# Transposing the softmax of two recurrent layers with 80 columns into two PSUM banks, and a new order of TensorE's work

## The chip, the cores and the metric

The kernel runs on one core of a Trainium2 chip. The metric is the device time of one execution in microseconds; a comparison is a median of several runs. Before the change it is 2704.88 us, the median of three runs (2704.35 to 2705.86).

A core has five engines that matter here. PE (TensorE) multiplies matrices: it holds a stationary matrix, streams the moving one through it column by column, and writes to PSUM. PSUM has eight banks of 512 fp32 columns and 128 partitions. ACT (ScalarE) and DVE (VectorE) read PSUM and write SBUF, the working memory. POOL (GpSimd) clears buffers here. SP issues most of the DMAs. Every engine works through its own queue in order and waits on semaphores for the others.

## What is computed

Two transformer layers on a sequence of 2048 rows of 576 values. Each has a recurrent attention and a gated feed-forward part. The attention goes through the sequence in 64 segments of 32 rows; each segment sees its own rows and 8 memory rows, which are the first 8 rows of the attention's output on the segment before.

```python
for s in range(n_seg):
    h = concat([mem, x[s*32:(s+1)*32]])            # 40 rows
    q, k, v = h @ Wq, h @ Wk, h @ Wv               # 32 heads of 128
    p = softmax(where(mask, q @ k.T * scale, -1e9))
    o = (p @ v) @ Wo
    mem = o[:8]
    outs.append(o[8:])
x = x + A(layernorm(x)); x = x + B(layernorm(x))   # twice, with the same weights
```

B is `(silu(x @ w1) * (x @ w3)) @ w2` with 4608 inner columns.

## The kernel before

**Steps.** The second layer follows the first by 8 segments (`LAG`). Step t works on segment t of layer 1 and segment t - 8 of layer 2, so there are 72 steps: 56 with both layers (`both(t)`), 16 with one. Where both run, the 40 + 40 columns of the two segments lie beside each other, and most products have 80 moving columns. `role(t)` alternates between 0 and 1 from step to step; with it alternates the order in which memory and rows of the two layers stand in the buffers.

**One step.** It is worked in four groups of eight heads (`GH`). For each group PE makes Q and K (letters Q and q: the 512 rows of the contraction, and the last 64), the scores (S), a transpose of the softmax's result (T), P times V (P), and the product with Wo (O and o). Between S and T, DVE and ACT make the softmax: mask added, maximum subtracted, exponential, sum, and P itself, which DVE writes to `PB` in bf16 (`sm_pb`). Keys of the two layers go to different columns of `PB`, its 128 columns being the 128 rows of the tile V; the queries of layer kind 0 are in partitions 0 to 39, those of kind 1 in 64 to 103. What `sm_pb` doesn't write is zero, since POOL clears a buffer of `PB` after its use (`pb_zero`).

**The transpose** (`ptr`) is a matmul: the stationary side is one head's `PB` (104 rows, 128 columns), the moving side is `fold`, a matrix of 104 x 40 with ones that send row r and row 64 + r to the same column. The eight heads' results, 128 keys x 40 queries, fill 320 columns of one bank. Each key row belongs to one of the layers, so nothing is added twice.

**The two copies** (`pt_ev`) bring it to SBUF, to `PTS`. Where both layers run, each copy reads all 320 columns and multiplies each partition by 0 or 1 (`slots`, four masks of 128 x 1): one copy keeps the key rows of one layer, the other those of the other. P times V (`pv`) then takes both halves as its 80 moving columns, `PTS[:, i, 0:2, 40 columns]`. Where one layer runs there is no mask, and the two copies take 160 columns each. There is one buffer of `PTS`, so a transpose comes after the P times V before it.

**V, feed-forward.** V of a step, or of two steps at once, is made between (letters X, x, V, v, G, g) and evicted in strips of 32 or 64 rows. The feed-forward part (F, f, W, w) of a block of 128 rows, for one or two layers, is spread over the four steps after the block, and fills PE where attention waits.

**The order** of PE is written out by hand in `ORDER`, one letter for each piece of work (`KINDS`): `FIRST` (16 steps), `FOUR` (4 steps, eleven times) and `LAST` (12 steps and the end). The function `plan` follows this order for PE. For the other engines it takes, at each point, the ready piece with the lowest priority number, by durations that stand in `make_nodes`; pieces marked "AD" go to ACT or to DVE, whichever it finds free first. It also gives out the buffers: a piece takes (`acq`) banks and SBUF buffers when it starts, and gives them back (`rel`) when their last reader has ended. Waits on the chip follow from the data and the buffers so chosen; the planner's times only choose.

**Tiling modes.** PE works either at full width, in two halves of 64 columns ("col"), in rows of 64 ("row") or in smaller tiles. Each letter has one or two modes that it can use; one that can use the mode of the letter before it keeps it. The transpose and P times V can be "full" or "col"; in "col" each matmul is issued as two of 64 stationary columns.

**The recurrence.** After the last o of a step ACT and DVE add the two halves of the last 64 output columns (`y_odd` writes one half to `YO` in fp32), write the next memory to `HT` (`y_mem`) and the outputs to `YTS` (`yts`). Four segments later POST transposes `YTS` for the residual addition.

A matmul of any letter is issued by `mm`, an ACT operation by `act`, a DVE operation by `v`: so the profile shows the helpers' lines, L591 for PE, L594 for ACT, L597 for DVE, and L1010 for POOL's clearing.

Of the kernel before, what the change touches and what calls it, by code (L numbers as in the profile page):

```python
# [38 lines left out]
def role(t):  # L39

    return (t - LAG) % 2
# [152 lines left out]
def ewh(*ns):  # L194
# [5 lines left out]
    "maQQQqqQqqSQqTqSqQQQqSSvVXxPTPTOPOTOoPooOoQqqqqQQSQqqvSVQQTQSqqPQOTSPoXTOPToxPOOooQqqqqQQSQQSvqVQTqqQSQqPSaOTPTO"  # L200
    "PTooPOOooQQqqqqQSQVvSqqQQQqqQTSSPXTOPTOPoToxPOOooQQpQqqVvqqSnQQSfFFqqfQQqSTQqfPFTWPSFTOOooPFTffPOOooWQqqqqQQFSQF"
    "SQffqVvqqQWTQSFxfqfQFSPXTWPFTfOPOTFPOOooooWQqfqQQSFQfqqVvSQqqfFWTQqfQSFPQqfTOSPFOTWPFTOPfoooOoFfqqQQQSWQqqvVSFfq"
    "qQQTWqqSQQPTSOoPbaOTXPxTOPooxOoXqqpQQQSVqqnQvfFSTQqqQQPSFfqqfQTFOPSWTFfPOOTFPWOooooffFQQQqqqWSGFfgqQQqfFSTQPQQqq"
    "qfFSWGTSfgGPFggTGOPOTFPOOooooWVvfqqQQQSFqqffFQQWTSFfqqQPQfqqSFQWTOfPSTaFoOPWOTFPffFOoooWQQqqqqQSbQgqqGSQQTQPQTgq"
    "qSGSOPGggTGPOTOPoooOoQqqppQQQSvqqVnnQQqqSFSffqTFQPQqWTFSPffOwTFPOTFPOWOwooooFffqqQQQSWwQFfgqqGSFqqfQQTWQPQSFffqq"
    "FGTgSwPGfggTGPFTOPOWOOowoooFqqfQQwWQaQfqqSFSvVfqqQFQTFqqfPQTQwSWFSfPOOTFPwTWffFPOOooooWwqqqQQQbSQqqgqGSQTQPQQqgq"
    "TSGSGPggGTOPOTOPoooOo"
)
FOUR = (
    "QqqpQQpQqqVvnSSnQFfqfqFQQQTfqqSFPWTFPSwTfFOOPWTwPOOooooFqqffQQQQfqqSFGSgqfFTQQPwQTQqqqgGSWPFGSfggfFOTGPOwTOPWOoo"  # L210
    "ooFqfqqQQwWQQVqvSaSFFffqqQQwQQqqSTWSFPffTFOPWwTOFPffTOFPwWOooooFfqqqQQWQQSqqqQSQQbQqgqSTGGPSgTGPOTggGPOTwPOOoooo"
)
LAST = (
    "QQpQqqqQSqQpnQqqVvTSSnQFffqqFPQTOwPoSWTffFPFTOPOOoooFqqqfQQwWQQfqfSFSFqGQQqqgTQQPWwFqgfTSSGGPFfggfFTGOPOTWPOOwoF"
    "oooFfqqfQQQwvSqqVQQWQqqSFTSqfqQPQWTOPSwFTFPffOTOwPWOooooFFqqffQQwQQqqvSWVSFqqfQQTWPQTqqSVQvPOSTbOPxwOoTooPOoXqQp"
    "QpqqvVQSQqqnQnSQQqqFTSfqfPQTOPSFTFPOWTOPwOooooFqffqQQQSQQqqqvVSTQQqqFSffqFPQWSwTFPffTOPFOTwPOOoWoooFqfqqQQQFSQfq"
    "xvXVwWSTFPQffqqQWQTSwFFPfqqQOSwWTFOPffTFPOWOwooooFQQvfqqVqqQSQWFSwFffqqQQQSTWQqPqTPSOTOPowOToboPxOoXqqqQQQpSvVqq"
    "qQQSnQTFfqQFSPfqQOSTFfPowTFPfOTOPFOfooowQQqqqfQQSqFSVvqqQwQFTSQffqqQPFTSXPwTOPOTFPOOooooFfxfVvqqQQQSQqqqfQSFQqqq"
    "QSTQwSPFTOffPFTOPwTOPfooOooFQqqqQQSqqqQQSQvVQTSfFQqqPwTFSPfTOFPOTOPoofOoopwFnfffFFwFwfffFFFwffFFwffFFwffFFwfFffF"
    "wFwfffFFFfww"  # L220
# [11 lines left out]
def make_nodes(em, nseg, pools, o=Opt, dma_bw=230e3, load_bw=400e3):  # L232
# [26 lines left out]
    ld_m0 = node("ACT", 0.1, em.load_m0(), prio=-90, name="m0", lat=2.5)  # L259
    ld_t = [load("ldt", kb(3 * R64, 4096), -10.0, em.load_tails(0)), node("ACT", 0.1, em.load_tails(1), prio=-120, name="ldt", lat=6.0)]  # L260
    node("ACT", 0.1, em.load_tails(2), prio=-80, name="ldt", lat=6.0)
# [48 lines left out]
    def v_nodes(name, t, k, prio, tail_at, emit, strips, deps, tail_deps, free):  # L310

        modes = ("col", "quad") if strips[0][3] == R64 else ("c32", "oct")
        b = banks()
        m_ = node("PE", 8 * 0.2158, emit(b, False), deps=deps, prio=prio, mode=modes[0], acq=b, name=name)
        n = node("PE", 0.2158, emit(b, True), deps=deps + tail_deps, prio=prio + tail_at, mode=modes[1], acq=b, name=name + "t")
        reads_ht.setdefault(t, []).extend([m_, n])
        for r in (0, 1):
            outs = em.v_parts(strips, r)
            b[r].users = len(outs)
            for p0, width, row, blk in outs:  # L320
                e = node("AD", (0.49, 0.6), em.v_ev(b[r], p0, width, row, blk), deps=[m_, n] + free.get(blk // 2, []), prio=prio + 0.01 * (blk // 2),
                         rel=[b[r]], name=name + "e")
                vx_ev.setdefault((name, t, blk // 2), []).append(e)
        return [m_, n]
# [16 lines left out]
    def vg_out(t, g, b, deps, row):  # L341

        return [node("AD", (0.49, 0.6), em.v_ev(b[r], row, R64, row, 2 * g + r), deps=deps, prio=t + o.vm + 0.01 * g + (0.05 if row == 0 else 0.0), rel=[b[r]],
                     name="VGe") for r in (0, 1)]

    def vx_pair(t, prio):

        if t and paired(t - 1):
            return
        deps = [ht_ready[li, s] for s in (t, t + 1) if 0 <= s < nst for li in layers_of(s) if s == t or li or not both(t)] + (ld_v if t <= 0 else [])  # L350
        free = {g: [pvs[t - 1, g]] for g in range(NG) if (t - 1, g) in pvs}
        for k in ((0, 1) if both(t) else (0,)):
            v_nodes("VX", t, k, prio + 0.01 * k, o.vxt, (lambda k: lambda b, tail: em.vx(t, k, b, tail))(k), em.vx_strips(t, k), deps, [], free)

    def step(t):
# [17 lines left out]
        for g in range(NG):  # L373
# [52 lines left out]
            me[f"SC{g}"], me[f"TR{g}"], me[f"PV{g}"], me[f"WO{g}"] = sc, tr, pv, wo  # L426
# [100 lines left out]
    def x_in(g):  # L527
        xn = Slot("xn")
        ld = node("DMA" if g else "ACT", 0.8 if g else 0.1, em.load_xn(g, xn), deps=reads_ht.get(4 * g - 3, [])[:1], prio=4 * g - 3.0 if g else -100, acq=[xn],
                  name="ldxn", lat=2.5)  # L530
# [37 lines left out]
class Emitter:  # L568
# [431 lines left out]
    def sm_pb(self, t, g, sme, pb):  # L1000
        def f(n):
            for kd, key, c0, w in self.p_at(t):
                rs = slice(64 * kd, 64 * kd + QW)
                X, rec = self.T.SME[rs, sme.i], self.T.STAT[rs, sme.i]
                self.v("tensor_tensor", self.T.PB[rs, pb.i, :, c0:c0 + w], X[:, :, key:key + w],
                       rec.unsqueeze(2).to_broadcast([QW, GH, w]), op=ALU.mult)
        return f

    def pb_zero(self, pb):
        return lambda n: self.ch("POOL", self.nc.gpsimd.memset(self.T.PB[:, pb.i], 0.0))  # L1010
# [101 lines left out]
    def yts(self, t, ls, tail):  # L1112
        def f(n):
            yT, _ = self.yT(t)
            for li in ls:
                j = (t - LAG * li) % 4
                c0 = self.ycol(t, self.kind(t, li), False)
                if not tail:
                    self.cp(n, self.T.YTS[:, li, 0:4, j * SEG:(j + 1) * SEG], yT[:, 0:4, c0:c0 + SEG])
                else:  # L1120
                    self.v("tensor_tensor", self.T.YTS[R64:P, li, 4, j * SEG:(j + 1) * SEG], yT[0:R64, 4, c0:c0 + SEG],
# [3 lines left out]
    def post_tr(self, li, g, b):  # L1125
        def f(n):

            for db in (4, 3, 2, 1, 0):
                d0 = min(db * P, D - P)
                self.mm(self.bk_bf(b, D)[:, d0:d0 + P], self.T.YTS[:, li, db, :], self.T.ident[:, 0:P], True, True, is_transpose=True)  # L1130
# [79 lines left out]
def kernel(  # L1210
# [41 lines left out]
    T.fold = sp.tile([P, QW], BF, name="fold")  # L1252

    T.slots = sp.tile([P, 2, 2], F32, name="slots")

# [29 lines left out]
    nc.gpsimd.memset(T.fold[:], 0.0)  # L1285
    for r in (0, R64):
        nc.gpsimd.affine_select(out=T.fold[:], in_=T.fold[:], compare_op=ALU.not_equal, fill=1.0, base=-r,
                                pattern=[[-1, QW]], channel_multiplier=1)

    nc.gpsimd.memset(T.slots[:], 0.0)  # L1290
    for e, kd, lo, hi in ((0, 1, 24, 80), (1, 0, 72, 112)):
        inside, outside = T.slots[:, e, kd:kd + 1], T.slots[:, e, 1 - kd:2 - kd]
        nc.gpsimd.memset(inside, 1.0)
        nc.gpsimd.affine_select(out=inside, in_=inside, compare_op=ALU.is_ge, fill=0.0, base=-lo, pattern=[[0, 1]], channel_multiplier=1)
        nc.gpsimd.affine_select(out=inside, in_=inside, compare_op=ALU.is_ge, fill=0.0, base=hi - 1, pattern=[[0, 1]], channel_multiplier=-1)
        nc.gpsimd.tensor_scalar(outside, inside, -1.0, 1.0, op0=ALU.mult, op1=ALU.add)

# [54 lines left out]
```

## Time and profile before

| | |
|---|---|
| median of three runs | 2704.88 us |
| the profiled execution | 2708.0 us |
| its span | 2705.0 us |
| granted TensorE clock, mean | 0.997 |
| PE busy | 2618.6 us |
| DVE busy | 2097.7 us |
| ACT busy | 1401.6 us |
| DMA, mean | 119 GB/s |

The span goes from the first to the last instruction of one profiled execution. A group of instructions is given as engine, operation, what it writes and reads, shape and count; behind the bar stand its busy time, the mean duration in ns, and the idle time of its engine just before, with what ended it. "PE bank L591 <- ACT PTS L594" in a list of waits means that PE stood until ACT had written `PTS`; behind it stand the sum, the number of times and the longest. A matmul's duration holds its way through the array (about 0.18 us even for 40 columns), and the next one starts long before its end: what PE needs for a piece is read from start to next start.

### The profile page before, as it was taken

What the parts mean: (1) busy time and instruction counts of PE and PEld (TensorE: products, weight loads), DVE (VectorE), ACT (ScalarE), POOL (GpSimd) and SP (SyncE); (2) the same over time, 40 slices, a digit from 0 to 9 for tenths busy, and PEclk for the clock granted to TensorE, in tenths of its full rate; (3) what the DMA queues carried; (4) which work ended last, traced back from release to release, by engine and by line L of the source; (5) the groups of instructions that cost most, each with busy time, mean ns of one, the idle gap of its engine ahead of it and who ended that gap; (6) DMA issues with size and microseconds to landing.
All of it is one profiled execution on the core that took longest, in us unless ns stands there. A gap on an engine that the chain in (4) does not pass through costs nothing.

```text
span 2705.0 us, 135792 instructions
## 1 busy us (share of the span) xinstructions
PE 2618.6 (97%) x60482; PEld 2272.3 (84%) x60523; DVE 2097.7 (78%) x5423; ACT 1401.6 (52%) x3978; POOL 334.1 (12%) x411
## 2 busy tenths in 40 slices
PE   5999999999999999999999999999999999999998
PEld 4788888888888888888888888888888888888886
DVE  5777887787788778777877877787777777777876
ACT  2655554554555555554555555455545546554452
POOL 1111110110111011011101101010111101011110
PEclk9999999999999999999999999999999999999999
DMA  9064524244342434434243433423343342334457
GB/s 316 7 182 118 158 82 128 80 119 116 104 124 85 116 90 119 117 108 128 76 119 88 127 108 108 134 80 110 94 124 106 108 139 70 112 93 130 129 166 245
DMA packets 478171, 321.99 MB, mean 119 GB/s; under 512 B 26024, under 2 KB 467760, under 8 KB 476944
## 3 DMA queue, kind: packets, MB, share of 16 engines
q1 hardware_dynamic: 474048, 305.43, 38.5%
q8 instruction: 473, 7.75, 1.2%
q0 software_dynamic: 3024, 6.93, 0.9%
q10 hardware_dynamic: 512, 0.94, 0.2%
q14 instruction: 114, 0.93, 0.1%
HBM read 308.49 MB, written 2.36 MB: 115 GB/s over the span
## 4 chain that ended last, share of the span: by engine, by line
PE 80%; DVE 9%; ACT 6%; issue 2%; DMA 2%; SPq 1%; POOL 0%; ACTq 0%; DVEq 0%; POOLq 0%
PE bank L591 80%; ACT V L594 3%; DVE STAT L597 2%; DVE PTS L597 2%; ACT PTS L594 1%; DVE V L597 1%; DVE SME L597 1%; DVE PB L597 1%; DMA W<-in_A_Wk_dram 1%; DVE HTT L597 1%; SPq L600 1%; DMA W<-in_B_w_dram 1%; ACT HT L594 0%; ACT QKT L594 0%; DMA WV<-in_A_Wv_dram 0%
## 5 line engine op out<-in xcount | busy, mean ns | idle before, releaser
L591 PEld LDWEIGHTS <-W 128*128 128x128 bf16 (+2 forms) x31904 | 1258.2, 100 | 128.8 <-issue 68.7
L591 PE MATMUL bank<-HT,W 128*128 128x80 bf16 (+3 forms) x23040 | 799.9, 196 | 16.8 <-issue 7.3
L591 PE MATMUL bank<-XTB,W 128*64 128x256 bf16 (+5 forms) x8864 | 662.6, 263 | 5.9 <-DMA W<-in_B_w_dram 3.0
L594 ACT ACTIVATE QKT<-bank 128x256 bf16<-128x256 f32 (+2 forms) x1524 | 349.5, 311 | 363.5 <-PE bank L591 320.7
L1010 POOL MEMSET PB<- 128x1024 bf16 x288 | 273.9, 951 | 1944.5 <-PE bank L591 1242.7
L591 PE MATMUL bank<-OT,WO 128*128 128x80 bf16 (+2 forms) x11520 | 401.6, 198 | 2.2 <-issue 1.8
L594 ACT ACTIVATE V<-bank 32x512 bf16<-32x512 f32 (+1 forms) x609 | 347.8, 586 | 90.4 <-PE bank L591 81.6
L591 PEld LDWEIGHTS <-WO 128*128 128x128 bf16 (+1 forms) x11520 | 376.8, 102 | 13.7 <-issue 4.4
L591 PE MATMUL bank<-WV,HT 128*32 128x512 bf16 (+5 forms) x3728 | 362.3, 381 | 3.8 <-issue 2.2
L591 PE MATMUL bank<-W2C,HTT 128*128 128x288 bf16 (+1 forms) x2776 | 318.4, 286 | 2.9 <-issue 1.8
L597 DVE TENSOR_REDUCE STAT<-SME 104x8 f32<-104x320 f32 (+1 forms) x576 | 274.0, 476 | 25.2 <-ACT SME L594 18.9
L597 DVE TENSOR_TENSOR PB<-SME,STAT 40x128 bf16<-40x128 f32 (+4 forms) x912 | 275.5, 336 | 9.7
L594 ACT ACTIVATE HTT<-bank 128x512 bf16<-128x512 f32 (+1 forms) x324 | 175.3, 550 | 185.9 <-PE bank L591 183.9
L591 PEld LDWEIGHTS <-HT 128*32 128x32 bf16 (+4 forms) x3768 | 164.1, 99 | 119.5 <-issue 20.3
L597 DVE SCALAR_TENSOR_TENSOR XR<-bank,XR 128x288 f32<-128x288 f32 x576 | 243.7, 448 | 23.3 <-PE bank L591 17.4
L591 PEld LDWEIGHTS <-HTT 128*128 128x128 bf16 (+1 forms) x2840 | 222.4, 103 | 42.2 <-issue 4.5
L597 DVE SCALAR_TENSOR_TENSOR HTT<-HTT,bank 128x512 bf16<-128x512 bf16 (+1 forms) x324 | 201.0, 620 | 59.0 <-ACT HTT L594 56.2
L594 ACT ACTIVATE OT<-bank 128x320 bf16<-128x320 f32 (+1 forms) x392 | 147.0, 403 | 173.0 <-PE bank L591 146.3
L597 DVE CAST QKT<-bank 128x192 bf16<-128x192 f32 (+4 forms) x524 | 140.5, 315 | 117.7 <-PE bank L591 117.3
L597 DVE TENSOR_TENSOR HTT<-HTT,bank 128x512 bf16<-128x512 bf16 (+1 forms) x324 | 203.6, 628 | 28.5 <-PE bank L591 0.9
L594 ACT ACTIVATE PTS<-bank,slots 128x320 bf16<-128x320 f32 x315 | 157.0, 531 | 128.8 <-PE bank L591 95.0
L594 ACT ACTIVATE SME<-SME 104x320 f32<-104x320 f32 (+1 forms) x288 | 135.5, 470 | 100.2 <-DVE SME L597 95.5
(69 smaller groups left out, 1856.8 us busy)
## 6 DMA issues: line engine op xcount, KB each, us to landing
W<-in_B_w_dram SPq DMA_DIRECT2D x612, 256.0 KB, 3.6
W2C<-in_B_w_dram SPq DMA_DIRECT2D x306, 288.0 KB, 3.3
W<-in_B_w_dram SPq DMA_DIRECT2D x612, 32.0 KB, 3.5
W<-in_B_w_dram SPq DMA_DIRECT2D x8, 1024.0 KB, 12.2
W<-in_A_Wq_dram SPq DMA_DIRECT2D x9, 512.0 KB, 9.5
WO<-in_A_Wo_dram SPq DMA_DIRECT2D x4, 1152.0 KB, 16.7
XR<-in_A_x_dram POOLq DMA_DIRECT2D x16, 288.0 KB, 2.8
WV<-in_B_w_dram SPq DMA_DIRECT2D x4, 1152.0 KB, 10.9
```

The lines of the kernel that those rows point to most:

```text
L591: self.ch("PE", self.nc.tensor.matmul(out, lhsT=lhsT, rhs=rhs, start=start, stop=stop, skip_group_check=True, **k))
L594: self.ch("ACT", self.nc.scalar.activation(*a, **k))
L597: self.ch("DVE", getattr(self.nc.vector, fn_)(*a, **k))
L600: self.ch("SP", self.nc.sync.dma_start(out=out, in_=in_))
L1010: return lambda n: self.ch("POOL", self.nc.gpsimd.memset(self.T.PB[:, pb.i], 0.0))
```

## The change

- `ptr`: where both layers run, the moving side is now a part of the identity, 80 columns in two runs of 40 (columns 0 to 39 and 64 to 103 of `ident`, in the order that the step's role asks for). Each head gives 128 x 80, four heads fill 320 columns of a bank, eight heads take two banks. Key rows of one layer have zeros for the other layer's queries, from the zeros of `PB`. Where one layer runs, it is 40 columns and one bank, as before.
- `pt_ev`: plain copies of 320 columns, one for each bank: two where both layers run, one where one does. `PTS` has the eight heads in a row, 80 columns each, so P times V reads one run of 80.
- `fold` and `slots` go, with their building on POOL. `YO` has no memory of its own any more: it lies in partitions 0 to 63 of two blocks of `YTS`, whose other half holds the last 64 output columns. `YTS` is indexed anew for it.
- The planner's numbers: the transpose of 80 columns 0.0358 us a head, the copies by the formula `ew(320)`, the copies of V on ACT 0.56 for 0.49, and for the loads at the start larger costs, longer delays and a "boot" piece ahead of them on the DMA queue.
- `ORDER` has the same letters, as many of each, in another sequence.

```diff
 FOUR = (
-    "QqqpQQpQqqVvnSSnQFfqfqFQQQTfqqSFPWTFPSwTfFOOPWTwPOOooooFqqffQQQQfqqSFGSgqfFTQQPwQTQqqqgGSWPFGSfggfFOTGPOwTOPWOoo"
-    "ooFqfqqQQwWQQVqvSaSFFffqqQQwQQqqqSTWSFPffTFOPWwTOFPffTOFPwWOooooFfqqqQQWQQSqqqQSQQbQqqgqSTGGPSgTGPOTggGPOTwPOOoooo"
+    "QpQqqqqQpQvVnSSQnQFqffqFTQQfqqSFPWTFPSwffTFOPOOTWPwOooooFqfqqQQQQqgfSWFSFGqfqQQTQPQqqgTSGwPGSFTgffgFGOPOTwPOWOoo"
+    "ooFqqffQQQFQWqqVvwSSFqqfQQQQqqTSWPwSTFffPFOTwOPWFffTFPOOwoWaoooFqfqQQWSqqqQQQQSbQQqqgqGSSTGPgTGPOTggOPGTOPwOoooo"
 )
...
-            bt = Slot("bank", users=2)
-            tr = node("PE", 8 * 0.0258, em.ptr(t, g, pb, bt), deps=[pbs], prio=pf + o.tr, mode="full/col", acq=[pts, bt], name="TR")
+            bt = banks(nl)
+            tr = node("PE", 8 * (0.0258 if nl == 1 else 0.0358), em.ptr(t, g, pb, bt), deps=[pbs], prio=pf + o.tr, mode="full/col", acq=[pts] + bt, name="TR")
...
-            pe_ = [node("AD", (0.425, 0.46) if nl == 2 else ew(160), em.pt_ev(t, g, m, bt, pts), deps=[tr], prio=pf, rel=[bt], name="PTe") for m in (0, 1)]
+            pe_ = [node("AD", ew(320), em.pt_ev(t, g, i, b, pts), deps=[tr], prio=pf, rel=[b], name="PTe") for i, b in enumerate(bt)]
...
     def ptr(self, t, g, pb, b):
 
         def f(n):
+            nq, v, e = self.nq(t), self.T.ident[0:104, 0:1], role(t)
+            I = bass.AP(v.tensor, v.offset + R64 * e, [list(x) for x in v.ap][:-1] + [[R64 - P * e, 2], [1, QW]]) if nq == SW else self.T.ident[0:104, 0:QW]
             for j in range(GH):
-                self.mm(self.bk(b)[:, j * QW:(j + 1) * QW], self.T.PB[0:104, pb.i, j, :], self.T.fold[0:104, :], True, True)
-        return f
-
-    def pt_ev(self, t, g, m, b, pts):
-
-        def f(n):
-            src = self.bk(b)[:, 0:GH * QW]
-            if not self.both(t):
-                w = 4 * QW
-                self.cp(n, self.T.PTS[:, pts.i, 0, m * w:(m + 1) * w], src[:, m * w:(m + 1) * w])
-                return
-            dst = self.T.PTS[:, pts.i, m, :]
-            keep = self.T.slots[:, role(t), m ^ role(t):(m ^ role(t)) + 1]
-            if n.by == "ACT":
-                self.act(dst, src, ACT.Copy, scale=keep)
-            else:
-                self.v("tensor_scalar", dst, src, keep, None, op0=ALU.mult)
-        return f
+                k = j * nq % (4 * SW)
+                self.mm(self.bk(b[j * nq // (4 * SW)])[:, k:k + nq], self.pbt(pb)[0:104, j, :], I, True, True)
+        return f
+
+    def pt_ev(self, t, g, i, b, pts):
+        return lambda n: self.cp(n, self.T.PTS[:, pts.i, 4 * SW * i:4 * SW * (i + 1)], self.bk(b)[:, 0:4 * SW])
...
-                        self.T.PTS[:, pts.i, 0:nq // QW, j * QW:(j + 1) * QW], True, True)
+                        self.T.PTS[:, pts.i, j * nq:(j + 1) * nq], True, True)
...
-    T.PTS = sp.tile([P, pools["pts"], 2, GH * QW], BF, name="PTS")
+    T.PTS = sp.tile([P, pools["pts"], GH * SW], BF, name="PTS")
...
-    T.YO = sp.tile([R64, 2 * QW], F32, name="YO")
-    T.YTS = sp.tile([P, 2, 5, P], BF, name="YTS")
+    T.YTS = sp.tile([P, 10, P], BF, name="YTS")
+
+    T.YO = T.YTS[0:R64, 8:10, :].rearrange("p a b -> p (a b)").bitcast(F32)[:, 0:2 * QW]
```

More of the change, by code (lines that the diff above doesn't have):

```diff
@@ L257, in load @@
         return node("DMA", nbytes / load_bw, fn, deps=deps, prio=prio, name=name, lat=2.0)
-    ld_m0 = node("ACT", 0.1, em.load_m0(), prio=-90, name="m0", lat=2.5)
-    ld_t = [load("ldt", kb(3 * R64, 4096), -10.0, em.load_tails(0)), node("ACT", 0.1, em.load_tails(1), prio=-120, name="ldt", lat=6.0)]
-    node("ACT", 0.1, em.load_tails(2), prio=-80, name="ldt", lat=6.0)
+    node("DMA", 4.0, lambda n: None, prio=-999.0, name="boot")
+    ld_m0 = node("ACT", 0.6, em.load_m0(), prio=-90, name="m0", lat=8.0)
+    ld_t = [load("ldt", 1.7 * kb(3 * R64, 4096), -10.0, em.load_tails(0)), node("ACT", 0.6, em.load_tails(1), prio=-120, name="ldt", lat=8.0)]
+    node("ACT", 0.6, em.load_tails(2), prio=-80, name="ldt", lat=10.0)
     ld_h = [load("ldqk", kb(512, 4096), half - 9.0, em.load_qk(half)) for half in (0, 1)]
@@ L320, in v_nodes @@
             for p0, width, row, blk in outs:
-                e = node("AD", (0.49, 0.6), em.v_ev(b[r], p0, width, row, blk), deps=[m_, n] + free.get(blk // 2, []), prio=prio + 0.01 * (blk // 2),
+                e = node("AD", (0.56, 0.6), em.v_ev(b[r], p0, width, row, blk), deps=[m_, n] + free.get(blk // 2, []), prio=prio + 0.01 * (blk // 2),
                          rel=[b[r]], name=name + "e")
@@ L353, in vx_pair @@
             v_nodes("VX", t, k, prio + 0.01 * k, o.vxt, (lambda k: lambda b, tail: em.vx(t, k, b, tail))(k), em.vx_strips(t, k), deps, [], free)
+    last_pt = []
     def step(t):
@@ L528, in x_in @@
         xn = Slot("xn")
-        ld = node("DMA" if g else "ACT", 0.8 if g else 0.1, em.load_xn(g, xn), deps=reads_ht.get(4 * g - 3, [])[:1], prio=4 * g - 3.0 if g else -100, acq=[xn],
-                  name="ldxn", lat=2.5)
+        ld = node("DMA" if g else "ACT", 0.8 if g else 0.6, em.load_xn(g, xn), deps=reads_ht.get(4 * g - 3, [])[:1], prio=4 * g - 3.0 if g else -100, acq=[xn],
+                  name="ldxn", lat=2.5 if g else 9.0)
         ht_set(0, g, ln_nodes("L0", xn, xn, [ld], 4 * g - 2.0 if g else -8, ht_writes(0, g)))
@@ L1004, in f, with pbt @@
                 X, rec = self.T.SME[rs, sme.i], self.T.STAT[rs, sme.i]
-                self.v("tensor_tensor", self.T.PB[rs, pb.i, :, c0:c0 + w], X[:, :, key:key + w],
+                self.v("tensor_tensor", self.pbt(pb)[rs, :, c0:c0 + w], X[:, :, key:key + w],
                        rec.unsqueeze(2).to_broadcast([QW, GH, w]), op=ALU.mult)
         return f
+    def pbt(self, pb):
+        return self.T.PB[:, pb.i]
     def pb_zero(self, pb):
-        return lambda n: self.ch("POOL", self.nc.gpsimd.memset(self.T.PB[:, pb.i], 0.0))
+        return lambda n: self.ch("POOL", self.nc.gpsimd.memset(self.pbt(pb), 0.0))
     def nq(self, t):
@@ L1129, in f @@
                 d0 = min(db * P, D - P)
-                self.mm(self.bk_bf(b, D)[:, d0:d0 + P], self.T.YTS[:, li, db, :], self.T.ident[:, 0:P], True, True, is_transpose=True)
+                self.mm(self.bk_bf(b, D)[:, d0:d0 + P], self.T.YTS[:, 4 * li + db if db < 4 else 8 + li, :], self.T.ident[:, 0:P], True, True, is_transpose=True)
         return f
@@ L1250 @@
     T.ident = sp.tile([P, P], BF, name="ident")
-    T.fold = sp.tile([P, QW], BF, name="fold")
-    T.slots = sp.tile([P, 2, 2], F32, name="slots")
     T.maskb = sp.tile([P, 2, QW], BF, name="maskb")
@@ L1284 @@
                             pattern=[[-1, P]], channel_multiplier=1)
[L1285 to L1296, printed above, removed]
     nc.gpsimd.memset(T.maskb[:], 0.0)
```

39 lines of the change are left out of this document (19 added, 20 removed).

## The prediction

> **What bounds the kernel now.** I read the page first, for the engine shares and the chain.
>
> ```profile
> span 2705.0 us, 135792 instructions
> PE 2618.6 (97%) x60482; PEld 2272.3 (84%) x60523; DVE 2097.7 (78%) x5423; ACT 1401.6 (52%) x3978; POOL 334.1 (12%) x411
> PE 80%; DVE 9%; ACT 6%; issue 2%; DMA 2%; SPq 1%; POOL 0%; ACTq 0%; DVEq 0%; POOLq 0%
> ```
>
> PE is busy 97% of the span and holds 80% of the chain; the rest of the chain are moments in which PE waited for a copy or a load. So a change counts in two ways only: the PE time that it adds, and the PE waits that it ends. Next the stretches: start, the 16 steps of FIRST, the eleven rounds of FOUR, most of LAST, and the end.
>
> ```profile
> 0.00:60.00 60.00, 32.70 (x760) 23.26 (x762) 28.73 (x74) 14.72 (x39) 11.57 (x34) 0.91 1.01 351
> 60.00:532.40 472.40, 455.43 (x11713) 390.01 (x11709) 372.15 (x993) 256.28 (x765) 65.89 (x75) 1.00 0.39 108
> 532.40:2260.50 1728.10, 1707.45 (x37864) 1497.64 (x37897) 1365.27 (x3498) 917.93 (x2564) 203.69 (x242) 1.00 0.38 108
> 2260.50:2640.00 379.50, 370.27 (x9209) 318.59 (x9210) 290.99 (x757) 193.63 (x562) 47.98 (x55) 1.00 0.43 125
> 2640.00:2705.00 65.00, 52.74 (x960) 42.86 (x952) 40.57 (x103) 19.00 (x53) 4.94 (x6) 0.97 0.74 239
> ```
>
> The columns are length, PE, PEld, DVE, ACT and POOL busy, granted clock, DMA share and GB/s. The first 60 us are full of DMA (share 1.01) and belong to the loads. In the middle 2580 us PE is idle for 17.0 + 20.7 + 9.2 = 47 us. Third, the waits: six of PE, and two between ACT and DVE.
>
> ```profile
> PE bank L591 <- issue: 15.3, 31, 2.2
> PE bank L591 <- ACT PTS L594: 12.3, 20, 1.9
> PE bank L591 <- ACT HT L594: 5.8, 17, 0.4
> PE bank L591 <- DVE PTS L597: 5.4, 20, 1.0
> PE bank L591 <- ACT V L594: 5.4, 15, 2.1
> PE bank L591 <- DVE PB L597: 2.6, 8, 0.5
> DVE PTS L597 <- ACT PTS L594: 53.5, 93, 2.5
> ACT PTS L594 <- DVE PTS L597: 24.4, 42, 1.1
> ```
>
> The largest named cause of PE's waits is exactly the pair of copies that is rewritten: 12.3 + 5.4 = 17.7 us over 40 waits. The last two rows tell why: 93 + 42 = 135 times the second copy's engine stood still until the first copy, on the other engine, had ended. The timeline shows one such place, which comes back in every round of FOUR.
>
> ```profile
> 1312.48 0.36 PE L591 MATMUL bank<-fold,PB 104*128 104x40 bf16 x8
> 1312.59 0.67 DVE L597 CAST V<-bank 64x512 bf16<-64x512 f32 x1
> 1312.69 1.14 PE L591 MATMUL bank<-W2C,HTT 128*128 128x288 bf16 x8
> 1313.29 0.55 DVE L597 TENSOR_SCALAR PTS<-bank,slots 128x320 bf16<-128x320 f32 x1
> 1313.88 0.53 ACT L594 ACTIVATE PTS<-bank,slots 128x320 bf16<-128x320 f32 x1 [0.56 <-DVE PTS L597]
> 1314.45 0.45 PE L591 MATMUL bank<-PTS,V 128*128 128x80 bf16 x8 [0.63 <-ACT PTS L594]
> 1314.74 3.15 PE L591 MATMUL bank<-OT,WO 128*128 128x80 bf16 x96
> 1314.80 0.44 ACT L594 ACTIVATE OT<-bank 128x320 bf16<-128x320 f32 x1 [0.39 <-PE bank L591]
> 1315.01 0.49 DVE L597 CAST OT<-bank 128x320 bf16<-128x320 f32 x1 [0.80 <-PE bank L591]
> ```
>
> The transpose (fold) ends; DVE copies, then ACT, never together; P times V starts 1.97 us after the transpose began. The two OT copies, which read two banks, do overlap (1314.80 to 1315.24 and 1315.01 to 1315.50).
>
> **The change, part by part.**
>
> *The transpose on PE.* Where both layers run (56 steps, 224 groups) it moves 80 columns for 40. No row shows such a transpose; the nearest is P times V, with as many matmuls of 80 columns.
>
> ```profile
> 1457.14 0.19 PE L591 MATMUL bank<-fold,PB 104*64 104x40 bf16 x1
> 1457.39 0.38 PE L591 MATMUL bank<-WV,HT 128*64 128x512 bf16 x1
> 1460.85 0.47 PE L591 MATMUL bank<-PTS,V 128*64 128x80 bf16 x15
> 1461.13 0.18 PE L591 MATMUL bank<-QKT 128*40 128x40 bf16 x1
> L591 PE MATMUL bank<-fold,PB 104*128 104x40 bf16 x1816 | 82.2, 180 | 2.8 <-DVE PB L597 2.3 <-POOL PB L1010 0.2
> L591 PE MATMUL bank<-fold,PB 104*64 104x40 bf16 x976 | 27.7, 186 | 0.1
> ```
>
> Start to next start, at full width 40 columns take 1312.69 - 1312.48 = 0.21 us and 80 take 1314.74 - 1314.45 = 0.29 (0.28 at most places). In halves of 64 columns they take 1457.39 - 1457.14 = 0.25 and 1461.13 - 1460.85 = 0.28. The counts are 1816/8 = 227 groups at full width and 976/16 = 61 in halves; walking the old order with the planner's rule that an operation keeps the mode before it puts 166 and 58 of them in two-layer steps. The cost is 166 x 0.075 + 58 x 0.03 = **+14.2 us**, all on PE. The new order has 143 and 81, which changes nothing, as both cost 0.28 at 80 columns. Bounds: 0 (the stationary side hides the columns) and 224 x 0.08 = 18. I take 14, since P times V is the same instruction but for 104 rows instead of 128.
>
> The Trainium skill ("TensorE: Matmul & The Clock Gate", Back-to-back issue gap) says that in a stream of weight loads and matmuls both set the spacing, about 81 ns at 128 columns. By that rule 80 columns would cost as much as 40 and the +14 would fall away. The trace is against it: 0.28 us for eight is 35 ns each, far under 81, and 40 columns take less than 80.
>
> *The two copies.* Their prices, and those of plain copies of the same shape and of the one-layer copies:
>
> ```profile
> L594 ACT ACTIVATE PTS<-bank,slots 128x320 bf16<-128x320 f32 x315 | 157.0, 531 | 128.8 <-PE bank L591 95.0 <-DVE PTS L597 23.7 <-ACT V L594 7.1
> L597 DVE TENSOR_SCALAR PTS<-bank,slots 128x320 bf16<-128x320 f32 x133 | 73.2, 550 | 41.0 <-ACT PTS L594 38.9 <-PE bank L591 0.6
> L594 ACT ACTIVATE OT<-bank 128x320 bf16<-128x320 f32 x299 | 122.2, 435 | 146.1 <-PE bank L591 119.9 <-DVE XR L597 22.5
> L597 DVE CAST OT<-bank 128x320 bf16<-128x320 f32 x149 | 72.6, 487 | 30.3 <-PE bank L591 28.0 <-ACT OT L594 1.2
> L594 ACT ACTIVATE PTS<-bank 128x160 bf16<-128x160 f32 x97 | 25.5, 303 | 28.7 <-PE bank L591 22.7 <-issue 2.8 <-DVE STAT L597 1.4
> ```
>
> Four things shorten the way from transpose to P times V. A plain copy takes 435 for 531 ns on ACT, 487 for 550 on DVE. From two banks both engines can copy at once, as with OT: the second ends about 0.49 us after its start instead of 0.53 + 0.55 after the first's. The first copy needs four heads only, 4 x 0.035 = 0.14 us sooner. And the first four heads of P times V need the first copy alone, where today each head needs both. At 1312.48 ACT was free, so its copy could have ended by about 1313.2 and DVE's (free at 1313.26) by 1313.75, in place of 1314.41: 0.65 us, about the whole 0.63 of the wait. PE's loss per wait is more than the idle row says: the product before it holds PE from 1312.69 to 1314.45, 1.76 us, where eight such take 1.01 undisturbed.
>
> ```profile
> 1506.49 1.17 PE L591 MATMUL bank<-W2C,HTT 128*128 128x288 bf16 x8
> 1507.50 0.36 PE L591 MATMUL bank<-fold,PB 104*128 104x40 bf16 x8
> ```
>
> That is 0.75 for an idle of 0.63, so the 40 waits hold 17.7 + 40 x 0.12 = 22.5 us. I take **-20 us**, as some places find both engines busy; ends 0 and -22.5.
>
> Why the copies exclude each other matters: the bank or the tile they write. OT is one tile too and its copies overlap, so it is the bank. The Trainium skill ("PSUM — Partial Sum Buffer", PSUM bank collisions raise a hardware error) agrees: two engines must be kept from one bank and quadrant at once, different banks are free. If instead the tile were the cause, only the shorter copies would count (a rival below).
>
> *One copy where one layer runs.* 64 groups: two copies (303 ns on ACT, one after the other) become one of 320 columns (435 or 487): some 0.2 us sooner. Their waits are among the 40.
>
> *Queues behind the copies.* The 53.5 + 24.4 = 78 us in which ACT or DVE stood at a copy hold back what is queued behind it in order (the softmax, the V and OT copies). PE's waits for V, PB and QKT fall with them. The V and PB rows above hold 8.0 us; I take **-3**, ends 0 and -8.
>
> *The new order.* Same letters, other places. By the mode rule PE changes its tiling 1067 times for 1081. A change costs 1501.83 - 1501.45 = 0.38 less the 0.25 of the same transpose without one, 0.13 us, and a little less where it follows long work: **-1.4**.
>
> ```profile
> 1501.45 0.45 PE L591 MATMUL bank<-fold,PB 104*64 104x40 bf16 x16
> 1501.83 2.24 PE L591 MATMUL bank<-XTB,W 64*128 64x256 bf16 x20
> ```
>  With such start-to-start durations I summed (an estimate) the PE work that lies between each producer and its consumer in one round of FOUR. Smallest gaps, old and new: scores to transpose 6.2 and 6.3 us, QK to scores 0.83 and 1.08, P times V to its product 0.74 and 0.98, transpose to P times V 0.98 and 0.98. The last has five gaps under 1.2 us for three, so the order spends part of the shorter way; the others are a little looser, **-2**, ends +10 and -10.
>
> *At no cost.* Building fold and slots leaves POOL's first 7 us, under the first loads (DMA share 1.01 to 60 us). YO now lies in unused rows of YTS, which the POST transposes read: its next write is most of a step (1728/44 = 39 us) later; were it to wait, 32 times 0.3 us on ACT, 9 us at most. The planner's new numbers (boot, lat, 0.56) act through the order and the choice of ACT or DVE only. At step 0 a tail comes ahead of the first QK, which drops 12 warming matmuls, under the weight loads: within 2 us either way.
>
> **The sum.** +14.2 - 20 - 3 - 1.4 - 2 = -12 us. The profiled execution took 2708.0 us (span 2705.0 and 3.0 around it), so 2696 for it; the timed runs lie 3.1 lower (median 2704.88): **2693**. Its own range, with these waits at -22.5 or at -13 and the order at -8 or at -2, is 2685 to 2700.
>
> **The rivals.**
> - *Queues count for more* (0.20). Once ACT and DVE no longer exclude each other, half of the 15.3 + 5.8 + 5.4 + 2.6 = 29 us that PE waits for issue, HT, V and PB goes too: 14 instead of the 3 + 2 taken, **2684**. For it: DVE at 78%, and 135 exclusions over 288 groups. Against: HT waits hang on the memory of the step before, which nothing here shortens.
> - *No change* (0.13). The new order uses up half of the waits it saves, 10 for 20: **2703**.
> - *Slower* (0.17). The transpose now asks for two of eight banks at once and PE stands at it until the V copies (0.67 us in the timeline, up to four to a bank) let one go; the wait of P times V moves to the transpose. For it: PE already waits 5.4 us for ACT V. From 13 us of waits that stay or come back it decides; with all of them back it is 14.2 - 1.4 = +13: **2718**. Against: the banks are held about 0.5 us shorter.
> - *Copies still one after the other* (0.03). Each of 40 waits loses 0.30 us (0.16 shorter, 0.14 earlier): 14.2 - 12 - 1.4 = +1, **2706**.
> - *The columns are free* (0.02), because weight loads set the spacing: **2679**.
>
> **How the numbers follow.** The forecast has 0.45. About 0.2% (5.4 us) is what a measurement can tell from no change: under 2699.5 is faster. Nearly all of the forecast, the first rival and the last give 0.65; no change, serial copies and the forecast's upper edge 0.17; slower 0.18. The range for 8 in 10 goes from 2676 (the first rival with 22.5 instead of 20 of the waits gone and the order worth 8 instead of 2) to 2712 (half of the slow case's +13; beyond it lies most of that case).
>
> **What would show it.** Transposes of 80 columns at 0.28 us for eight; PTS copies at 435 and 487 ns, and the rows of ACT PTS and DVE PTS waiting for each other gone; PE's waits for PTS under 5 us; PE busy up by about 13. A long PE wait at the transpose for a V copy, or PE waits for PTS above 12 us, would prove me wrong.

## The result, and the profile after

The changed kernel takes 2700.32 us (median of 16 runs, 2695.9 to 2704.96) beside 2704.64 (16 runs, 2701.29 to 2709.18): a ratio of 0.9983, 95% interval 0.9975 to 0.9990, or 4.3 us (2.7 to 6.8). It is faster, but the forecast was -12. The profiled execution has a span of 2696.5 us and took 2698.3. That is 2.0 under the median, while the old kernel's profiled one (2708.0) lay 3.4 over its own: the two profiles are 9.7 us apart where the medians are 4.3 apart.

The first lines of the page of the changed kernel, as read before:

```profile
span 2696.5 us, 137303 instructions
PE 2626.7 (97%) x61164; PEld 2281.5 (85%) x61202; DVE 2104.4 (78%) x5345; ACT 1359.6 (50%) x3992; POOL 334.4 (12%) x399
PE 71%; DVE 4%; ACT 2%; DMA 1%; issue 1%; SPq 1%; POOL 0%; DVEq 0%; ACTq 0%; POOLq 0%
```

The largest rows in the list of PE's waits of the changed kernel (sum in us, times, longest):

```profile
PE bank L594 <- DVE XN L600: 13.5, 1, 13.5
PE bank L594 <- ACT HT L597: 7.6, 18, 1.6
PE bank L594 <- issue: 7.5, 9, 2.7
PE bank L594 <- DMA W<-in_A_Wk_dram: 7.5, 6, 2.8
PE bank L594 <- ACT V L597: 4.2, 4, 1.9
PE bank L594 <- DVE HTT L600: 3.6, 11, 0.4
PE bank L594 <- DVE YTS L600: 3.4, 13, 0.8
PE bank L594 <- ACT PTS L597: 3.3, 7, 0.7
PE bank L594 <- DVE PTS L600: 1.8, 2, 1.5
PE bank L594 <- ACT QKT L597: 1.6, 5, 0.5
PE bank L594 <- DMA W<-in_B_w_dram: 1.5, 4, 0.7
PE bank L594 <- DVE PB L600: 1.3, 3, 0.5
```

The waits for PTS fell from 17.7 to 3.3 + 1.8 = 5.1 us, those for issue from 15.3 to 7.5. HTT and YTS, which hardly stood in the old list, hold 7.0. In the list of all engines the two rows in which ACT and DVE waited for each other's PTS copy (78 us) are gone. The groups of the rewritten pieces:

```profile
L597 ACT ACTIVATE PTS<-bank 128x320 bf16<-128x320 f32 x344 | 144.8, 441 | 130.2 <-PE bank L594 116.5 <-ACT V L597 4.2 <-ACT OT L597 2.2
L600 DVE CAST PTS<-bank 128x320 bf16<-128x320 f32 x168 | 81.1, 483 | 30.8 <-PE bank L594 22.4 <-ACT V L597 4.0 <-ACT HTT L597 0.8
L594 PE MATMUL bank<-ident,PB 104*128 104x80 bf16 x1144 | 65.2, 201 | 0.4 <-DVE PB L600 0.4
L594 PE MATMUL bank<-ident,PB 104*64 104x80 bf16 x1296 | 40.2, 202 | 0.0
```

The copies cost 441 and 483 ns. 1144/8 = 143 transposes run at full width and 1296/16 = 81 in halves, as the walk through the new order had it. At the end of a round of FOUR, in the timeline of the changed kernel (start, duration, idle before):

```profile
1312.92 0.45 PE L594 MATMUL bank<-ident,PB 104*128 104x80 bf16 x8
1313.20 1.31 PE L594 MATMUL bank<-OT,WO 128*128 128x80 bf16 x32
1313.52 0.44 ACT L597 ACTIVATE PTS<-bank 128x320 bf16<-128x320 f32 x1
1313.85 0.49 DVE L600 CAST PTS<-bank 128x320 bf16<-128x320 f32 x1
1314.35 0.45 PE L594 MATMUL bank<-PTS,V 128*128 128x80 bf16 x8
...
1317.97 1.31 PE L594 MATMUL bank<-HT,W 128*128 128x80 bf16 x32 [0.34 <-ACT HT L597]
...
1319.07 0.28 DVE L600 TENSOR_TENSOR YTS<-bank,YTS 64x32 bf16<-64x32 f32 x2 [0.51 <-ACT YTS L597]
...
1319.50 0.44 PE L594 MATMUL bank<-ident,YTS 128*128 128x128 bf16 x5 [0.22 <-DVE YTS L600]
```

The transpose takes 1313.20 - 1312.92 = 0.28 us, the copies overlap (1313.85 to 1313.96), and P times V begins 1.43 us after the transpose, with no idle time, where it was 1.97 and a wait. But behind the first QK of the next round POST now waits for YTS, which it did not in the old order.

The stretches of the changed kernel (length, PE, PEld, DVE, ACT, POOL busy, clock, DMA share, GB/s); its rounds of FOUR lie from 531.8 to 2260.9:

```profile
0.00:60.00 60.00, 28.84 (x581) 19.94 (x583) 27.45 (x65) 13.74 (x34) 9.03 (x21) 0.86 0.99 350
60.00:531.80 471.80, 461.15 (x11993) 400.12 (x11995) 372.27 (x1000) 251.42 (x738) 66.31 (x76) 0.98 0.38 107
531.80:2260.90 1729.10, 1715.93 (x38391) 1500.26 (x38424) 1372.11 (x3432) 883.75 (x2630) 204.27 (x243) 1.00 0.38 108
2260.90:2640.00 379.10, 372.58 (x9307) 320.68 (x9308) 294.03 (x751) 193.61 (x549) 49.86 (x56) 1.00 0.45 131
```

The eleven rounds, two thirds of the time, gained nothing: 1729.1 for 1728.1 us. PE's idle time there fell from 20.7 to 13.2, and its busy time rose by 8.5. Following the letters through both traces, the 100th letter begins at 97.7 us for 90.4, 7.3 late; from there to the end of FIRST 7.9 us are won, in FOUR 1.0 lost, and from its end to the end of the trace 8.9 won. The late start goes with the clock, which is 0.86 and 0.98 in the first two rows (0.91 and 1.00 before).

### The profile page after: what moved, and what is told of

The parts are those of the page before. It is cut to its first block, busy times and chain, and to the rows that moved or that the text cites. A ratio compares the mean times of both kernels' runs of the same rounds, so it can differ in the third digit from the quotient of the medians.

```text
span 2696.5 us, 137303 instructions
## 1 busy us (share of the span) xinstructions
PE 2626.7 (97%) x61164; PEld 2281.5 (85%) x61202; DVE 2104.4 (78%) x5345; ACT 1359.6 (50%) x3992; POOL 334.4 (12%) x399
## 4 chain that ended last, share of the span: by engine, by line
PE 71%; DVE 4%; ACT 2%; DMA 1%; issue 1%; SPq 1%; POOL 0%; DVEq 0%; ACTq 0%; POOLq 0%
PE bank L594 71%; DMA W<-in_B_w_dram 1%; DVE HTT L600 1%; ACT V L597 1%; SPq L603 1%; DVE STAT L600 1%; DVE PB L600 1%; DVE SME L600 1%; ACT PTS L597 0%; ACT YTS L597 0%; DVE V L600 0%; DVE PTS L600 0%; ACT SME L597 0%; ACT QKT L597 0%; DVE HT L600 0%
## 5 line engine op out<-in xcount | busy, mean ns | idle before, releaser
L597 ACT ACTIVATE QKT<-bank 128x64 bf16<-128x64 f32 (+2 forms) x1648 | 377.3, 314 | 338.5 <-PE bank L594 324.7
L594 PE MATMUL bank<-OT,WO 128*128 128x80 bf16 (+3 forms) x11520 | 408.1, 198 | 1.7
L594 PEld LDWEIGHTS <-WO 128*128 128x128 bf16 (+1 forms) x11520 | 382.0, 102 | 25.0 <-issue 13.7
L597 ACT ACTIVATE V<-bank 32x512 bf16<-32x512 f32 (+1 forms) x556 | 318.3, 586 | 142.5 <-PE bank L594 134.3
L594 PE MATMUL bank<-WV,HT 128*32 128x512 bf16 (+4 forms) x3772 | 372.5, 387 | 7.3 <-issue 2.7
L594 PE MATMUL bank<-W2C,HTT 128*64 128x288 bf16 (+1 forms) x3184 | 324.8, 286 | 0.5 <-issue 0.4
L594 PEld LDWEIGHTS <-HT 128*32 128x32 bf16 (+5 forms) x3808 | 163.6, 101 | 122.5 <-issue 24.9
L594 PEld LDWEIGHTS <-HTT 128*64 128x64 bf16 (+1 forms) x3248 | 229.0, 105 | 35.5 <-issue 3.9
L600 DVE CAST V<-bank 64x512 bf16<-64x512 f32 (+1 forms) x308 | 211.1, 686 | 46.1 <-PE bank L594 39.3
L597 ACT ACTIVATE OT<-bank 128x320 bf16<-128x320 f32 (+1 forms) x413 | 154.5, 408 | 144.6 <-PE bank L594 139.7
L597 ACT ACTIVATE PTS<-bank 128x320 bf16<-128x320 f32 x344 | 144.8, 441 | 130.2 <-PE bank L594 116.5
```

The costliest lines, as they stand in the source:

```text
L594: self.ch("PE", self.nc.tensor.matmul(out, lhsT=lhsT, rhs=rhs, start=start, stop=stop, skip_group_check=True, **k))
L597: self.ch("ACT", self.nc.scalar.activation(*a, **k))
L600: self.ch("DVE", getattr(self.nc.vector, fn_)(*a, **k))
```

## The experiments

Each is compared with the old kernel by a ratio, both run on the same chip; the changed kernel's is 0.9983 (0.9975 to 0.9990). The groups of runs come from different chips, so between groups the ratios say more than the medians.

**The two halves of the change, apart.** The sections of the order are interchangeable, as each has the same letters. First the new transposes and copies with the old order throughout (the three strings of `ORDER` taken from the old kernel).

> The changed kernel with the whole old order: transposes and copies alone. The prediction's theory: PE's waits for PTS (17.7 us) fall under 5, PE work grows by 14, and the sum is -5 to -10: 2695 to 2700. Rival (banks): an order made for one bank makes the transpose wait for a second; PE's waits at the transpose grow by 10 or more and the time is over 2706.

2741.28 us (4 runs), ratio 1.0136 (1.0120 to 1.0151). The rival was right, and by far. The waits for PTS are gone (2.2 and 1.3 us remain), but a new one leads the list of PE's waits, and its timeline shows where:

```profile
PE bank L594 <- DVE HTT L600: 22.6, 36, 1.5
```

```profile
1254.97 0.68 DVE L600 SCALAR_TENSOR_TENSOR HTT<-HTT,bank 128x512 bf16<-128x512 bf16 x1
1255.22 0.31 PE L594 MATMUL bank<-ident,PB 104*128 104x80 bf16 x4
1255.63 0.44 ACT L597 ACTIVATE PTS<-bank 128x320 bf16<-128x320 f32 x1
1255.75 0.69 DVE L600 TENSOR_TENSOR HTT<-HTT,bank 128x512 bf16<-128x512 bf16 x1
1256.49 0.30 PE L594 MATMUL bank<-ident,PB 104*128 104x80 bf16 x4 [0.96 <-DVE HTT L600]
```

The first four heads go to a free bank; the other four stand 0.96 us, until the feed-forward part's multiplication on DVE has let go of the second. In the rounds no wait for PTS is left, so the new transposes and copies end these waits without the new order, too. A round takes 159.6 us, against 157.1. FIRST also ends 12 us later than in the old kernel (544.7 for 532.4).

Then the other half: the old kernel with the new order.

> The old kernel with the new order: the order alone. If the new order leans on the shorter way through the copies (five gaps from transpose to P times V under 1.2 us in a round of FOUR, three before), PE's waits for PTS grow from 17.7 us to 25 or more, and with the 7 us lost at the start the time is 2712 or more. Rival: the order brings the gain whatever the transposes do, and without their 14 us of PE work the time is under 2695.

2772.8 us (4 runs), ratio 1.0250 (1.0236 to 1.0264), as the first theory had it, and more.

```profile
PE bank L591 <- DVE PTS L597: 14.3, 54, 1.3
PE bank L591 <- ACT PTS L594: 11.1, 27, 1.0
PE bank L591 <- DVE PB L597: 9.3, 22, 1.8
```

The waits for PTS grow from 17.7 to 25.4 us: the new order leaves so little between transpose and P times V that the old copies don't fit. The idle rows show only a part of it: in the rounds, from start to next start, P times V takes 16.6 us more than in the changed kernel, and the products just ahead of it (W2, Wo, QK) 23.5 more, of 42.6 by which the rounds are longer. A round takes 161.1 us. Each half alone loses 36 or 67 us; together they win 4.

**Only FIRST.** The changed kernel with the old FIRST.

> The changed kernel with the old FIRST; FOUR and LAST stay new. The changed kernel lost 7 us before the 100th letter and won 8 us from there to the end of FIRST. If the 8 us come from the transposes and copies, they stay and the 7 come back: about 2693. If they come from the new places of the letters, they go as the 7 come back: about 2700.

2708.53 us (11 runs), ratio 1.0013 (1.0004 to 1.0022), outside both. The start was as early as in the old kernel (100th letter at 91.3 us), but FIRST ended at 544.1, 12 us later, while FOUR and LAST were as in the changed kernel (157.0 a round). So what the changed kernel wins inside FIRST hangs on the order made for two banks. A small part of the 12 us may be the clock, which stood at half for 24 us between the 100th letter and the end of FIRST, in the old kernel for none; the median of the runs' mean clocks is that of the changed kernel (0.993).

**The added work on PE.**

```diff
-                self.mm(self.bk(b[j * nq // (4 * SW)])[:, k:k + nq], self.pbt(pb)[0:104, j, :], I, True, True)
+                self.mm(self.bk(b[j * nq // (4 * SW)])[:, k:k + QW], self.pbt(pb)[0:104, j, :], self.T.ident[0:104, 0:QW], True, True)
```

> The changed kernel with transposes of 40 moving columns everywhere; the queries of the second 40 columns are left out, so their part of PTS is stale. This takes the added PE work away (14 us by the prediction's step) and leaves the rest. If PE bounds all the way, a round of FOUR falls by 16 x 0.07 = 1.1 us, to 156.1, and the time by 12 to 15 us, to 2686 to 2688. Rival: softmax and copies set the pace too and the rounds keep 157 us; then under 5 us, 2696 or more.

2690.19 us (5 runs), ratio 0.9939 (0.9927 to 0.9952): 10 us under the changed kernel by the medians, 12 by the ratios. A round takes 156.3 us, 0.9 less. The wider transposes cost nearly what the prediction set, though a little under its 12 to 15.

**The two engines at once.**

```diff
-            pe_ = [node("AD", ew(320), em.pt_ev
+            pe_ = [node("ACT", ew(320)[0], em.pt_ev
```

> The changed kernel with both copies of PTS given to ACT. If it is the two engines at once that end the waits for PTS, these come back (over 10 us, from 5.1) and the time rises by 5 or more, over 2705. Rival: the shorter copies and the earlier first copy are enough, ACT has room at 50% busy, DVE is relieved, and the time stays within 2 us of 2700 or falls.

2703.57 us (11 runs), ratio 0.9992 (0.9983 to 1.0001). Between the two. PE's waits for PTS stay at 3.9 us, so the shorter and earlier copies and the order are enough to end them; still the time is some 2 to 3 us worse, and a round 157.6 us for 157.2. PE now waits longer for ACT's copies of V (7.7 us for 4.2). That both engines can copy is worth something, but not by the wait that I had in mind.

**The start.** In the trace's clock records of the changed kernel the clock stands at half for 34 us of the first 130, in the old kernel for 10. Taking the distance from matmul to matmul there against that of the same shape elsewhere, matmuls lost 8.4 us by it, in the old kernel 1.2, which would be the whole 7.2 us that the start came late. That sum hangs on which distances are taken for one matmul's, and the runs with the fill, below, put the clock's share nearer to half. First suspect were 12 warming matmuls, which `qk` issues only when it comes ahead of its tail; here they are put into `qk_tail` as well:

```diff
     def qk_tail(self, t, u, b):
...
             first = self.begin(b)
+            for c in range(4 if first and t == 0 and u % 4 == 0 else 0):
+                for _ in range(3):
+                    self.mm(self.bk(b[1])[:], self.T.ident[:, 0:P], self.T.W[:, 4 + c, u * 512:(u + 1) * 512], True, True)
```

> The changed kernel with the 12 warming matmuls of the first QK group put back, ahead of the tail that now comes first. Its trace had the clock granted at half for 34 us in the first 130 us, the old kernel's for 10 us, and stood 7 us behind at the 100th letter. Theory A (the clock): without the warming matmuls PE waits for each weight chunk with one matmul of work, and the clock falls; with them back, half-clock time at the start falls under 15 us, the 100th letter comes 6 to 8 us sooner, and the time is 2692 to 2695. Theory B (the places of the letters in FIRST lose the 7 us): within 2 us of the changed kernel, 2698 to 2702.

2697.31 us (11 runs), ratio 0.9969 (0.9960 to 0.9978), but in the profiled execution not by the way of theory A: half clock was at 37 us and the 100th letter at 98.6. The other executions differ from it. Five of the eleven had a mean clock of 0.995 or more and took 2694.1 to 2696.5 us; the other six, the profiled one (0.992) among them, took 2697.3 to 2702.1. Of the changed kernel's 16 runs one had such a clock (2696.9 us). The lower median goes with those five; whether the warming matmuls brought their clock is not shown.

Then more such products, where PE waits for the weights of V and for the first copies:

```diff
+    def fill(self, b, n):
+        for _ in range(n):
+            self.ch("PE", self.nc.tensor.matmul(self.bk(b)[:], lhsT=self.T.ident[:, 0:P], rhs=self.T.W[:, 4, 0:512], start=True, stop=True, skip_group_check=True))
...
     def pv(self, t, g, pts, b):
         def f(n):
             nq = self.nq(t)
+            self.fill(b[0], 6 if t == 0 and g < 2 else 0)
...
         sets = [(b, strips, self.begin(b)) for b, strips in sets]
+        self.fill(sets[0][0][0], 6 if t == 0 and sets[0][2] else 0)
```

> The warm-start kernel with 24 more products of 512 columns at step 0, where PE waits for weights and copies anyway (six ahead of each of the two V tails and of the first two P times V). In the changed kernel PE ran at half clock for 34 us of the first 130 us, and its matmuls there took 8.4 us longer than at full clock (old kernel: 10 us and 1.2). Theory A (PE's idling at the start lowers the clock): half-clock time falls to 15 us or less, the 100th letter comes 5 to 7 us sooner than in the changed kernel (97.7), the time is 2690 to 2694. Theory B (the half-clock windows follow from something else, as from the kind of work): they stay, and the time is 2697 to 2702.

2696.29 us (5 runs, 2696.0 to 2697.21), ratio 0.9964 (0.9952 to 0.9977). Half clock fell to 17 us, the 100th letter came at 93.6 and FIRST ended at 525.7, 6.1 us sooner. The time is 4 us under the changed kernel, but only 1 under the kernel with the warming matmuls, on which it builds; the profiled execution gave 4 back at the end, where it had 10 us of half clock for under 1. The stretch from 40 to 68 us, first the changed kernel, then this one:

```profile
40.00:68.00 28.00, 20.21 (x451) 15.07 (x452) 12.55 (x31) 9.31 (x23) 3.52 (x4) 0.63 0.78 267
```

```profile
40.00:68.00 28.00, 25.18 (x582) 16.66 (x585) 15.56 (x40) 10.43 (x27) 3.52 (x4) 0.94 0.79 269
```

PE is busy 5 us more, and the clock is 0.94 for 0.63. It varies between executions: the kernel with both copies on ACT, whose start is unchanged, had 17 us of half clock in its profile, too. So three profiles with the fill (17, 10 and 7 us, below) stand against four with this start without it (34, 37, 37 and 31) and the one at 17. The mean clocks of all runs go the same way: 0.995 to 0.998 in the 17 runs of the three kernels with the fill, 0.990 to 0.997 in the 49 of the five without it (medians 0.992 to 0.994). That the fill raises the clock is well supported; that PE's idling is what lowers it stays likely, not shown. Nor is the new start alone in it: the changed kernel with the whole old order had 31 us of half clock, too.

How much of the late start is the clock's can be read from the ninth transpose, which stands at the 100th letter. It begins at 97.4 us in the changed kernel and at 89.8 in the old one. With both copies on ACT, without any added product and at 17 us of half clock, it begins at 94.0; with the fill and POST later (below), at 10 us, as in the old kernel, at 93.4. So about 4 of the 7.6 us go with the clock, and the rest stays without it. PE's first matmul comes at 13.5 us for 10.5, and the first transpose at 36.9 for 35.2; how that rest divides is open.

**The old kernel with the fill.**

> The old kernel with the same 24 products at the waits of step 0. Its trace had 10 us of half clock at the start, 1.2 us of loss. Theory A (idling lowers the clock, the old order idles no less but was caught less): little to win, 2703 to 2705. Rival (the fill helps any order, the traced execution of the old kernel was a lucky one): 2700 or less.

2707.95 us (11 runs), ratio 1.0013 (1.0004 to 1.0022): slower, by 3.5 us, which neither had expected. Half clock at the start was 7 us in its profile, for 10. The old order had nothing to win there; where the loss comes from was not found.

**POST later.**

```diff
-    "QpQqqqqQpQvVnSSQnQFqffq
+    "QQqpqqqQpQvVnSSQnQFqffq
```

> The changed kernel with the POST transposes one letter of Q and one of q later in each round of FOUR (QQqpqqqQp for QpQqqqqQp). In the changed kernel PE waits 0.38 us in each round for YTS there. If this wait is paid in full, a round takes 156.8 us instead of 157.2 and the time falls by 4 us, to 2696. Rival: the next wait (the S that waits for HTT, 0.43 us) or the lost cover takes it back: within 1.5 us of 2700.

2697.43 us (6 runs), ratio 0.9967 (0.9956 to 0.9979): 3 us by the medians, 4 by the ratios. In the rounds the wait for YTS is gone and a round takes 157.0 us on average, two of them 156.6. That is 0.2 us a round, the 2.4 us over eleven rounds that the changed kernel's list holds there, and not the 0.38 of the expectation. So the rounds account for some 2 us; the time came near to the expected 2696, and where the rest comes from is open.

**Both.** POST later and the fill.

> The fill kernel with POST later, both edits together. If the start and the wait at POST are separate, they add: fill was 2696.3 and POST later 3 to 4 us, so 2692 to 2694 and half-clock time in the first 130 us near 17 us again. If fill's lower half-clock time was chance (another run without fill had 17 us as well), the first 130 us have 30 us or more again and the time is 2696 to 2698.

2690.32 us (5 runs, 2687.7 to 2692.87), ratio 0.9951 (0.9937 to 0.9964): 13 us under the old kernel, and the best of all that compute the whole. Within the intervals the gains add: the ratios of the two edits make 0.9948 together. A round takes 156.7 us. The first 130 us have 10 us of half clock. In its rounds of FOUR one row of PE waits is left:

```profile
PE bank L594 <- ACT HT L597: 3.8, 11, 0.3
```

It is the recurrence: the first QK of a round waits for the memory that the last o of the step before has made.

**A transpose ahead of a product with Wo.**

```diff
-gTGPOTgg
+gTGPTOgg
```

> best1 with one transpose moved ahead of one product with Wo in each round of FOUR (GTPTOGG for GTPOTGG, in the middle of the last step), where PE waits 0.31 us for the OT copies behind a V copy. If the transpose covers the wait, a round falls by 0.2 to 0.3 us and the time by 2 to 3 us against best1. Rival: the transpose finds no two free banks or its P not ready, and a round is 0.2 us or more longer.

2695.92 us (7 runs), ratio 0.9973 (0.9962 to 0.9983). The rival: a round takes 157.25 us, 0.56 more than in the kernel before it, and PE now waits at the transposes, in the rounds 22 times for over 0.1 us, 3.4 us in all. The timeline shows one place:

```profile
2084.95 1.69 ACT L597 ACTIVATE V<-bank 64x512 bf16<-64x512 f32 x3
2086.21 0.30 PE L594 MATMUL bank<-ident,PB 104*128 104x80 bf16 x4
2086.69 0.30 PE L594 MATMUL bank<-ident,PB 104*128 104x80 bf16 x4 [0.18 <-ACT V L597]
```

The second four heads start when ACT's copies of V end (2086.64). The transpose doesn't read V, so what it waits for is the bank.

## Why the prediction was wrong, step by step

The direction was right, and so were the price of the transposes and the end of the waits for PTS. The sum was too large by 7 us: two steps failed, the new order and the start.

- *The transpose, +14.2.* Right in its row (0.28 us for eight). Taken out, it gave 10 to 12 us. That 80 columns cost as much as 40, the rival by a rule of the Trainium skill ("TensorE: Matmul & The Clock Gate", Back-to-back issue gap), falls.
- *The two copies, -20.* The waits went as forecast, the term was a little too large. The copies take 441 and 483 ns, no longer exclude each other, and the waits fell by 17.7 - 5.1 = 12.6 us over 40 - 9 = 31 waits; with the 0.12 us each that the idle rows don't show, 16 us. What stayed lies almost wholly outside the rounds of FOUR. That the copies wait by bank, not by tile, holds: PTS is one tile still, and they overlap. Of the four things that were to shorten the way, two engines at once was not needed for this: with both copies on ACT 3.9 us were left. And only 9.3 of the 17.7 us lay in the rounds, which hold 44 of the 56 steps with both layers and so some 11 of the 14 us of added work. There the two terms nearly cancel, which the prediction, by its sum over the whole, did not see.
- *Queues, -3.* V and PB fell by 1.2 + 1.3 = 2.5 us.
- *The new order, -2.* **This step failed.** It compared the gaps from transpose, scores and QK, and left out POST and the banks that the feed-forward part holds. In the rounds of FOUR the waits for PTS, V and issue (9.3 + 2.1 + 1.7 us) went; waits for HTT and YTS came in their place:

```profile
PE bank L594 <- ACT HT L597: 4.1, 12, 0.3
PE bank L594 <- DVE HTT L600: 2.9, 8, 0.4
PE bank L594 <- DVE YTS L600: 2.4, 11, 0.2
PE bank L594 <- DMA W<-in_B_w_dram: 0.3, 2, 0.2
```

  The scores are what waits for HTT; they don't read it, so it is a bank that they wait for. That is 9.7 us of idle for 17.5, and the rounds' added work (11 times about 0.9 us by the kernel with 40 columns) took the rest. Moving POST alone gave 3 to 4 us back, 2 of them in the rounds; the waits for HTT were not tried.
- *"At step 0 ... within 2 us either way."* **This step failed, too**, by 7 us in the profiled execution, as much as the whole sum is off. I had priced the dropped matmuls by the loads that cover them, and left the clock out. PE's busy time in the first 60 us fell from 32.7 to 28.8 us, and the clock of the stretch from 0.91 to 0.86. About 4 us go with the clock; the other 3 stay with the new order of the start, and their cause is open.
- *The rivals.* "No change" (2703) lies nearer to 2700.3 than the forecast does, and for the rounds it was right: the new order's waits and the added work took what the copies gave. "Slower" named a real mechanism, two banks at once, but with the old order the holder is the feed-forward's DVE work, not the copies of V that I had named; these show in the last experiment, where one letter is moved. With the old order it costs 36 us net. The new order is what keeps it away, so the order was not the side matter of -2 that I took it for: without it the change loses. "Queues count for more" has the fall of issue from 15.3 to 7.5 on its side; the gain of 8.9 us in LAST, which I had not set apart, is neither the code's nor the order's alone. LAST took 444.5 us before, about 440.5 with the new code and the old order, about 447 with the old code and the new order, and 435.6 with both; in the eight other profiles with both it took 1.5 to 6.1 us longer than that.

With the start and POST mended, the kernel is at 2690.3, 13 us under the old one, where the sum of the prediction stood at 2693. That the two lie so near is partly luck, as no term of the sum stands for the added products.

## What to carry to other kernels

A hand-made order and the code that it was made for are one thing: each half of this change lost 36 to 67 us alone. Who forecasts a new order must list every producer with its consumer, the holders of the banks among them, and not only those around the edit; the wait that goes is often paid at the next letter. Waits are to be summed by stretch, as the added work is, and read from start to next start, since the idle rows show only a part. And a change of what PE does while the first weights load is to be priced by the granted clock of the stretch, beside the waits.

## What the runs showed of the hardware

The clock's records stand at half in pieces of 3.4 us (up to 13.7 in one) after stretches in which PE had idled (it was busy for at most 83% of the 3.4 us before each), and the same kernel differs in it from execution to execution. The 16 runs of the changed kernel had mean clocks of 0.992 to 0.996 and times over 9 us; the five runs of the kernel with the fill lay within 1.2. That is no rule: with the same fill and POST later they spread over 5.2 us, with the moved transpose over 7.5, at mean clocks of 0.996 to 0.998. In halves of 64 columns, transposes of 40 columns took almost as long as those of 80 (0.25 and 0.28 us for eight heads), at full width 0.21 and 0.28.
